# Which queue issues the score gathers: SyncE and GpSimd trade their DMAs, and the pacing copies go

## The chip, the cores and the metric

One core of one Trainium2 chip. The metric is the device time of the whole program in microseconds (us); the profiled execution also gives the span from its first to its last recorded instruction. TensorE, VectorE, ScalarE, GpSimd and SyncE are PE, DVE, ACT, POOL and SP in the profile.

## What is computed

Attention with talking heads (4 batches, 12 heads, 448 positions, head size 64), and behind it a bilinear feed-forward block on 1792 tokens (768 to 1536 and back):

```python
scores = scale * np.matmul(q, k.transpose(0, 1, 3, 2))
scores = np.einsum('bhij,hg->bgij', scores, w_pre)
scores = scores - np.max(scores, axis=-1, keepdims=True)
attn = np.exp(scores)
attn = attn / (np.sum(attn, axis=-1, keepdims=True) + 1e-09)
attn = np.einsum('bhij,hg->bgij', attn, w_post)
attn_out = np.matmul(attn, v)
a = x @ w_a
b = x @ w_b
return a * b @ w_out
```

## The kernel before, in words

**Chunks and units.** A batch's 448 queries are cut into chunks of 120, 120, 120 and 88. For a chunk, `qk` (L249) multiplies q and k head by head, and ACT copies each pair of heads from PSUM into the score tile `s` of the chunk (L266): query on the partition, then head, then key. Six such copies fill a chunk. The pool `big` holds two `s` tiles, so the copies for chunk c overwrite the tile of chunk c-2.

A chunk is then worked off in units of 20 queries (23 units a batch, 92 in all, numbered from 0). Mixing the heads wants head and query together on the partition, so `gather` (L271) moves 5 queries by 12 heads from `s` to 60 partitions of a tile `sb` by a DMA inside SBUF: four DMAs of 105 KB for a unit of 20. Each `sb` tile has AH + 1 = 4 buffers.

**A step** works on unit s: `premix` (L292; PE, 8 matmuls of L303), maximum and exponential (`smax`), the row sums' reciprocal folded into the second mixing weights (`norm`; L320 to L326), and `postmix` (L347) for unit s-1, whose transposed result ACT copies out (L357). Into the steps come, by a table made ahead (`items` and `after`, filled in the loop over `chunks` behind `av`), the `qk` pairs of the next chunk, the multiplication with v (`av`, L371) of a finished group of 8 units, the store of its result to `xd` (L381), the loads, and `spread_q` (L219; POOL reorders the q just loaded). At the head of step s, `gather(s + 3)` is issued. The first `qk` of a chunk comes three units ahead of the first unit of the chunk before it, so one step behind the issue of the last gather of the tile that it overwrites. Behind a batch's last chunk, which has five units, that step (s = 15, 38 and 61) has two `qk`.

**Queues.** Each engine takes its instructions in the program's order, DMA issues among them. SP issues all gathers, the first batch's k, the first two chunks' q, and the stores; POOL issues v, and the later k and q. A DMA completes on one of eight semaphores, which a queue's DMAs use in turn, so a queue has at most eight DMAs under way. `pace` (L122) puts one small POOL copy into each step that waits for `rs` of the unit before; what POOL issues behind it waits too.

Behind step 83 the feed-forward block's weights are loaded and converted (`load_raw` L433, L450 to L456), first beside the last units, then beside its matmuls (L494 to L496), which run to the end.

Of the kernel before, what the change touches and what calls it, by code (L numbers as in the profile page):

```python
# [7 lines left out]
F32 = mybir.dt.float32  # L8
# [13 lines left out]
def talking_heads_bilinear_kernel(  # L22
# [11 lines left out]
    nc = tc.nc  # L34
    B, _, G, S = k.shape
    H, D = 2 * G, 64
# [5 lines left out]
    QG = 3  # L42
# [49 lines left out]
    const = ctx.enter_context(tc.tile_pool(name="const", bufs=1))  # L92
# [23 lines left out]
    def ps_t():  # L116
        return ps.tile([128, 2, 512], F32, tag="t", name="pst", bufs=1)[:, 0]

    tick = const.tile([128, 1], F32, name="tick")
    seen = {}  # L120

    def pace(u):  # L122

        if u in seen:
            nc.gpsimd.tensor_copy(tick[:60], seen.pop(u)[:60, :1])  # L125

    todo_at, now = {}, [0]

    def later(fn, n=3):
        todo_at.setdefault(now[0] + n, []).append(fn)  # L130
# [56 lines left out]
    kt, qraw, qt, vt = {}, {}, {}, {}  # L187
    st, sbt, mt, at, ant, ptt, pps, xps = {}, {}, {}, {}, {}, {}, {}, {}

    def load_v(b, i):  # L190

        g, slot = divmod(i, V_PARTS)
        if slot == 0:
            vt[b, g] = v_p.tile([128, H // 2, R, D], F32, tag=f"v{g}", name="v")
        runs = [(2 * C * slot, 0, 2 * C)] if slot < R - 1 else [(2 * C * slot, 0, C), (2 * C * slot, C, C)]
        for s0, p0, n in runs:
            while n:
                r, p = divmod(s0, P)
                m = min(n, P - p)
                nc.gpsimd.dma_start(out=vt[b, g][p0:p0 + m, :, slot], in_=v[b, g][p:p + m, :, r])  # L200
                s0, p0, n = s0 + m, p0 + m, n - m

    def load_k(b, i):
        t = k_p.tile([128, S], F32, tag="k", name="k")
        (nc.sync if b == 0 else nc.gpsimd).dma_start(out=t, in_=k[b, :, i])
        kt[b, i] = t

    def load_q(c, j):
        b, t0, n = chunks[c]
        t = q_p.tile([128, QG, CHUNK], F32, tag="qraw", name="qraw", bufs=3)[:, :, :n]  # L210
        sl = slice(G * t0 + QG * j * n, G * t0 + QG * (j + 1) * n)
        (nc.sync if c < 2 else nc.gpsimd).dma_start(out=t, in_=q[b, :, sl].rearrange("d (h t) -> d h t", h=QG))
        qraw[c, j] = t

    def cut(n):
# [52 lines left out]
    def halves(n):  # L268
        return [(o, min(QH, n - o)) for o in range(0, n, QH)]

    def gather(u):  # L271
        c, o, n = units[u]
        sbt[u] = [sb_p.tile([128, S], F32, tag=f"sb{e}", name="sb") for e in range(2)]
        for i, (t, m) in enumerate(halves(n)):
            r = 64 * (i // 2)
            nb = chunks[c][2] // QB
            k_ = (o + t) // QB
            r0 = 64 * (t % QB // QH)
            if k_ < nb:
                rows = st[c][r0:r0 + QH * nb].rearrange("(i k) h s -> k i h s", k=nb)[k_]  # L280
            else:
                rows = st[c][r0 + QH * nb:r0 + QH * nb + m]
            nc.sync.dma_start(out=sbt[u][i % 2][r:r + m * H], in_=rows)

    def blocks_of(u):
        n = units[u][2]
        return [(u, j, min(QB, n - QB * j)) for j in range(2) if n > QB * j]

    def rows_of(n):
        return 64 + (n - QH) * H if n > QH else n * H  # L290

    def premix(u):  # L292
        n = units[u][2]
        tiles = sbt.pop(u)
        for k_ in blocks_of(u):
            mt[k_[:2]] = ps.tile([128, 512], F32, tag="m", name="mp")[:, :S]
        for i in (0, 2, 1, 3):
            if i >= len(halves(n)):
                continue
            m = halves(n)[i][1] * H  # L300
            r, col = 64 * (i // 2), 64 * (i % 2)
            M = 64 if n == QU or i == 0 else m
            nc.tensor.matmul(mt[u, i // 2][col:col + M], lhsT=wp[r:r + m, :M], rhs=tiles[i % 2][r:r + m])  # L303
# [12 lines left out]
    def norm(k_):  # L316
        u, j, n = k_
        m = rows_of(n)
        a, rs = at.pop((u, j))
        nc.vector.tensor_scalar(rs[:m], rs[:m], 1e-9, None, op0=ALU.add)  # L320
        if j == 0 and m > 64:
            seen[u] = rs
        rc = w_p.tile([128, 1], F32, tag="rc", name="rc", bufs=4)
        nc.vector.reciprocal(rc[:m], rs[:m])
        kr = w_p.tile([128, H, QB], F32, tag="kr", name="kr", bufs=5)
        nc.vector.tensor_scalar(kr[:m], kf[:m], rc[:m], None, op0=ALU.mult)  # L326
        ant[u, j] = a, kr
# [21 lines left out]
    def evac_p(k_):  # L349
        u, j, n = k_  # L350
        if (u, j) not in pps:
            return
        a = group_of[u]
        o = (u - groups[a][1]) * QU + j * QB
        if a not in ptt:
            ptt[a] = big.tile([128, R, H, AVC], F32, tag="pt", name="pt")
        nc.scalar.copy(ptt[a][:, :, :, o:o + n], pps.pop((u, j))[:, :, :, :n])  # L357
# [28 lines left out]
    for c in range(1, NC):  # L386
        b, t0, _ = chunks[c]
# [14 lines left out]
    for a in range(NA - 1):  # L402
        b, u0, n = groups[a]
# [6 lines left out]
    def open_moe():  # L410
        short.close()
        mo["c"] = ctx.enter_context(tc.tile_pool(name="mc", bufs=2))
        mo["w"] = ctx.enter_context(tc.tile_pool(name="mw", bufs=2))

    def load_x(b, parts=(0, 1, 2)):
        if b not in xt:
            xt[b] = big.tile([128, 2, KD, S], F32R, tag="s" if b < 2 else "pt", name="xhl")
        for i in parts:
            nc.sync.dma_start(out=xt[b].bitcast(F32)[:, 1, 2 * i:2 * i + 2], in_=xd[b][:, 2 * i:2 * i + 2])
# [10 lines left out]
    def load_raw(u):  # L430
        kind, i, e = u
        t = mo["c"].tile([128, CW, 2], I32, tag="raw", name="raw")
        nc.sync.dma_start(  # L433
            out=t.rearrange("p (k f) t -> p k (f t)", k=KD), in_=(w_ab if kind == "f" else w_out)[i, e].bitcast(I32)
        )
        raws[u] = t
# [115 lines left out]
    def take(it, n):  # L552
        for _ in range(n):
            next(it, None)
# [30 lines left out]
    def tail_ops():  # L585
        x0 = split_ops(0)
        first = conv_ops(range(2))
        for i in range(XS):
            next(first, None)
            yield  # L590
        for _ in first:
            next(x0, None)
            yield
        yield from x0

    with tc.manual_schedule():
# [30 lines left out]
        for s in range(NU + 2):  # L627
            now[0] = s
            if s == last_prep + 1:
                open_moe()  # L630
                load_raw(order[0])
                later(lambda: load_raw(order[1]), 1)
                for i in range(3):
                    later(lambda i=i: load_x(0, (i,)), 2 + i)
                tail = tail_ops()
            if s == NU - 2:
                load_x(1)
            if s == NU - 1:
                load_x(2)
            while nxt_g <= min(s + AH, NU - 1) and ready.get(units[nxt_g][0], -1) < s:  # L640
                gather(nxt_g)
                nxt_g += 1
            pace(s - 1)
            if s in (2, 4):
                for i in range(V_PARTS):
                    load_v(0, V_PARTS * (s // 2 - 1) + i)
            b, i = divmod(s, NUB)
            if b + 1 < B and 0 <= i - V_AT < 2 * V_PARTS:
                load_v(b + 1, i - V_AT)
            for fn in todo_at.pop(s, ()):  # L650
                fn()
            if s < NU:
                premix(s)
            if s >= 2:
                for k_ in blocks_of(s - 2):
                    evac_p(k_)
            if s < NU:
                for k_ in blocks_of(s):
                    smax(k_)
            pairs = [it for it in items.get(s, ()) if it[0] is qk]  # L660
            for it in items.get(s, ()):
                if it not in pairs[1:]:
                    it[0](*it[1:])
            if s < NU:
                for k_ in blocks_of(s):
                    norm(k_)
            if 0 <= s - 1 < NU:
                postmix(blocks_of(s - 1))
            for it in pairs[1:]:
                it[0](*it[1:])  # L670
            for it in after.get(s, ()):
                it[0](*it[1:])
            if s >= last_prep + 2:
                take(tail, RATE if s < NU - LATE else RATE2)
            if s == NU:
                for _ in tail:
                    pass
                tail = split_ops(1)
                for k_ in blocks_of(NU - 1):
                    evac_p(k_)  # L680
                run_a(0, 0)
            if s == NU + 1:
                run_b(0, 0)
# [59 lines left out]
        for j in range(B * KD):  # L743
            b, m = divmod(j, KD)
# [57 lines left out]
```

## Time and profile before

| | |
|---|---|
| median of 3 runs | 989.19 us (988.44 to 990.23) |
| the profiled execution | 987.99 us |
| its span | 986.2 us |
| PE busy | 926.3 us (94%) |
| DVE, ACT, POOL busy | 512.9, 412.1, 325.5 us |
| granted TensorE clock, mean | 0.973 |

PE is busy for most of the span; in a kernel like this what can be won or lost lies in the stretches in which PE waits, and in those in which its granted clock is low. So the profile is read by stretches: where PE idles, who ended that wait, and what that one waited for. A wait in the trace is put down to the semaphore that came last; as DMAs share semaphores in turn, a gather's landing can carry the name of a store.

### The profile page before, as it was taken

The numbers are of one execution on the slowest core, as the hardware profiler recorded it, in microseconds if no ns is written. First come the engines' busy times: TensorE is split into PE (matmuls) and PEld (weight loads), VectorE is DVE, ScalarE is ACT, GpSimd is POOL, SyncE is SP. The second block draws the span as 40 slices with busy tenths as digits, with TensorE's granted clock in tenths as the row PEclk, the third lists the DMA queues.
The fourth block names the chain that finished last, engine by engine and source line by source line (L and its number), as shares of the span: only waits on it lengthen the run. The fifth ranks groups of instructions, "written<-read, shape, count | busy, mean of one in ns | idle before, by whom it ended". The sixth has DMA issues, their size and how long they took to land.

```text
span 986.2 us, 20021 instructions
## 1 busy us (share of the span) xinstructions
PE 926.3 (94%) x7852; PEld 748.3 (76%) x7852; DVE 512.9 (52%) x1100; ACT 412.1 (42%) x851; POOL 325.5 (33%) x399
## 2 busy tenths in 40 slices
PE   7599699979987999979899999999999999999998
PEld 4256366646654666658799999999999999999997
DVE  3365356545654556674887555656655363341500
ACT  3467577656765768743311111111111043443521
POOL 2544113411243012020334323233332244554642
PEclk9899799989998999989999999999999999999999
DMA  4545334553355334464435424234242276656432
GB/s 143 148 146 178 123 129 146 163 161 124 127 156 189 113 132 138 148 210 157 139 133 160 146 109 150 109 140 148 96 147 109 86 259 228 223 179 246 156 124 70
DMA packets 64637, 147.60 MB, mean 150 GB/s; under 512 B 6892, under 2 KB 49024, under 8 KB 63520
## 3 DMA queue, kind: packets, MB, share of 16 engines
q1 hardware_dynamic: 58528, 131.11, 38.7%
q0 software_dynamic: 6016, 15.21, 5.7%
q8 instruction: 63, 1.03, 0.4%
q14 instruction: 30, 0.25, 0.1%
HBM read 81.01 MB, written 26.74 MB: 109 GB/s over the span
## 4 chain that ended last, share of the span: by engine, by line
PE 77%; DMA 14%; DVE 2%; ACT 2%; issue 1%; SPq 0%; POOL 0%; ACTq 0%; DVEq 0%
DMA sb<-s 9%; PE pp L347 9%; PE mp L303 7%; PE po L495 6%; PE po L496 6%; PE po L494 6%; PE xp L371 6%; PE pa L494 6%; PE pa L495 6%; PE pa L496 6%; PE pb L496 5%; PE pb L495 5%; PE pb L494 5%; PE pst L243 5%; DMA xd<-xs 4%
## 5 line engine op out<-in xcount | busy, mean ns | idle before, releaser
L347 PEld LDWEIGHTS pp<-kr,a 124*64 124x64 f32 (+1 forms) x2520 | 134.1, 139 | 47.4 <-ACT pt L357 43.9
L312 DVE TENSOR_REDUCE nm<-mp 124x1 f32<-124x448 f32 x180 | 104.3, 619 | 114.1 <-PE mp L303 112.8
L347 PE MATMUL pp<-kr,a 124*64 124x120 f32 (+1 forms) x2520 | 150.9, 272 | 3.2 <-DVE kr L326 1.7
L456 POOL TENSOR_TENSOR cvm<-cvm,cvr 128x768 int32<-128x768 int32 x36 | 66.9, 1858 | 213.3 <-DVE cvm L455 205.4
L313 ACT ACTIVATE a<-mp,nm 124x448 f32<-124x448 f32 x180 | 112.7, 631 | 56.9 <-DVE nm L312 56.8
L243 PE MATMUL pst<-k,q 64*64 64x448 f32 (+1 forms) x744 | 97.3, 575 | 38.7 <-ACT s L266 37.5
L484 POOL TENSOR_TENSOR wl<-rawo,wh 128x768 fp32r<-128x768 f32 x48 | 93.1, 1962 | 100.8 <-ACT wh L483 100.8
L506 ACT COPY sa<-pa 128x448 f32<-128x448 f32 x48 | 25.6, 533 | 223.5 <-PE pa L496 215.2
L357 ACT COPY pt<-pp 128x480 f32<-128x480 f32 x180 | 93.6, 579 | 43.9 <-PE pp L347 43.8
L266 ACT COPY s<-pst 124x896 f32<-124x896 f32 (+1 forms) x93 | 84.1, 904 | 60.6 <-DMA sb<-s 36.5
L125 POOL COPY tick<-rs 60x1 f32<-60x1 f32 x92 | 16.8, 183 | 280.5 <-DVE rs L320 280.5
L303 PE MATMUL mp<-sb,wp 60*64 60x448 f32 x720 | 101.0, 578 | 8.5 <-ACT a L313 5.4
L495 PE MATMUL pa<-xhl,wh 128*128 128x448 f32 x288 | 105.3, 366 | 1.9 <-DVE xhl L426 1.9
L494 PE MATMUL pa<-xhl,wh 128*128 128x448 f32 x288 | 105.3, 366 | 0.0
L495 PE MATMUL po<-hl,wh 128*128 128x448 f32 x288 | 104.5, 363 | 0.7 <-DVE hl L531 0.7
L496 PE MATMUL pa<-xhl,wl 128*128 128x448 f32 x288 | 105.0, 365 | 0.0
L494 PE MATMUL po<-hh,wh 128*128 128x448 f32 x288 | 104.4, 362 | 0.0
L496 PE MATMUL po<-hh,wl 128*128 128x448 f32 x288 | 104.4, 362 | 0.0
L496 PE MATMUL pb<-xhl,wl 128*128 128x448 f32 x282 | 102.3, 363 | 0.9 <-POOL wl L484 0.9
L494 PE MATMUL pb<-xhl,wh 128*128 128x448 f32 x282 | 102.2, 362 | 0.0
L495 PE MATMUL pb<-xhl,wh 128*128 128x448 f32 x282 | 102.2, 362 | 0.0
L531 DVE TENSOR_TENSOR hl<-hl,hh 128x448 fp32r<-128x448 f32 x48 | 57.5, 1252 | 75.8 <-ACT hh L530 75.8
(72 smaller groups left out, 1378.5 us busy)
## 6 DMA issues: line engine op xcount, KB each, us to landing
sb<-s SPq DMA_DIRECT2D x356, 105.0 KB
raw<-in_w_ab_dram SPq DMA_DIRECT2D x24, 768.0 KB
rawo<-wod SPq DMA_DIRECT2D x24, 768.0 KB
hd<-hf SPq DMA_DIRECT2D x48, 224.0 KB
raw<-in_w_out_dram SPq DMA_DIRECT2D x12, 768.0 KB
xhl<-xd SPq DMA_DIRECT2D x12, 448.0 KB
hl<-hd SPq DMA_DIRECT2D x4, 1344.0 KB
out_dram<-so SPq DMA_DIRECT2D x24, 224.0 KB
```

The lines of the kernel that those rows point to most:

```text
L243: nc.tensor.matmul(out[64 * e:64 * e + cols.stop - cols.start], lhsT=qt[c, i // QG][rows, i % QG, cols], rhs=kt[b, i][rows],)
L266: nc.scalar.copy(st[c].rearrange("p (g i) s -> p i g s", g=2)[:m, i], sp[:m])
L303: nc.tensor.matmul(mt[u, i // 2][col:col + M], lhsT=wp[r:r + m, :M], rhs=tiles[i % 2][r:r + m])
L312: nc.vector.tensor_reduce(nm[:m], mp[:m], axis=AXX, op=ALU.max, negate=True)
L313: nc.scalar.activation(a[:m], mp[:m], ACTF.Exp, bias=nm[:m], scale=1.0, accum_out=rs[:m])
L347: nc.tensor.matmul(o, lhsT=lhsT, rhs=rhs)
L357: nc.scalar.copy(ptt[a][:, :, :, o:o + n], pps.pop((u, j))[:, :, :, :n])
L456: lambda: nc.gpsimd.tensor_tensor(m, m, r, op=ALU.add),
L484: nc.gpsimd.tensor_tensor(ll[:, sl], raw, hh.bitcast(F32)[:, sl], op=ALU.subtract)
L494: nc.tensor.matmul(o, lhsT=hh[:, k0 + kk], rhs=mh[:, kk], start=(kk == 0), stop=False)
L495: nc.tensor.matmul(o, lhsT=hh[:, k0 + kk], rhs=ml[:, kk], start=False, stop=False)
L496: nc.tensor.matmul(o, lhsT=ll[:, k0 + kk], rhs=mh[:, kk], start=False, stop=(kk == n - 1))
```

## The change

POOL issues all gathers. SP issues every load of v, k and q. `pace` and its copies are gone, with the tile `tick` and the notes in `norm` that it used.

```diff
-    tick = const.tile([128, 1], F32, name="tick")
-    seen = {}
-
-    def pace(u):
-
-        if u in seen:
-            nc.gpsimd.tensor_copy(tick[:60], seen.pop(u)[:60, :1])
-
...
-                nc.gpsimd.dma_start(out=vt[b, g][p0:p0 + m, :, slot], in_=v[b, g][p:p + m, :, r])
+                nc.sync.dma_start(out=vt[b, g][p0:p0 + m, :, slot], in_=v[b, g][p:p + m, :, r])
...
-        (nc.sync if b == 0 else nc.gpsimd).dma_start(out=t, in_=k[b, :, i])
+        nc.sync.dma_start(out=t, in_=k[b, :, i])
...
-        (nc.sync if c < 2 else nc.gpsimd).dma_start(out=t, in_=q[b, :, sl].rearrange("d (h t) -> d h t", h=QG))
+        nc.sync.dma_start(out=t, in_=q[b, :, sl].rearrange("d (h t) -> d h t", h=QG))
...
-            nc.sync.dma_start(out=sbt[u][i % 2][r:r + m * H], in_=rows)
+            nc.gpsimd.dma_start(out=sbt[u][i % 2][r:r + m * H], in_=rows)
...
-        if j == 0 and m > 64:
-            seen[u] = rs
...
-            pace(s - 1)
```

On POOL, from the first q reordering in the set-up into the first steps, before:

```order
L226 COPY q<-qraw 128x3x60 x2
L212 DMA qraw<-in_q_dram 128x360
L226 COPY q<-qraw 128x3x60 x2
L125 COPY tick<-rs 60x1 x2
L200 DMA v<-in_v_dram 112x6x64
L200 DMA v<-in_v_dram 16x6x64
L200 DMA v<-in_v_dram 96x6x64
```

and now (the changed kernel's lines have other numbers: L275 is the gather's DMA, L218 the reordering of q, L192, L197 and L204 load v, k and q, L371 is the store):

```order
L218 COPY q<-qraw 128x3x60 x2
L275 DMA sb<-s 60x1x448 x16
L218 COPY q<-qraw 128x3x60 x2
L275 DMA sb<-s 60x1x448 x8
L218 COPY q<-qraw 128x3x60 x2
L275 DMA sb<-s 60x1x448 x12
L218 COPY q<-qraw 128x3x60 x2
```

The reorderings of q (`COPY q<-qraw`) now stand between gathers, and no load and no pacing copy is left on POOL.

On SP, over the first stores of a finished group, before:

```order
L283 DMA sb<-s 60x1x448 x64
L381 DMA xd_84<-xs 128x3x160
L283 DMA sb<-s 60x1x448 x8
L381 DMA xd_84<-xs 128x3x160
L283 DMA sb<-s 60x1x448 x17
```

and now:

```order
L204 DMA qraw<-in_q_dram 128x360
L192 DMA v<-in_v_dram 80x6x64
L192 DMA v<-in_v_dram 48x6x64
L371 DMA xd_84<-xs 128x3x160
L197 DMA k<-in_k_dram 128x448 x2
L192 DMA v<-in_v_dram 64x6x64 x2
L204 DMA qraw<-in_q_dram 128x360
L197 DMA k<-in_k_dram 128x448
L371 DMA xd_84<-xs 128x3x160
```

A store that waits for its data now holds up loads; before it held up gathers.

The semaphores that POOL's first gathers wait for, now (DMASW0 to DMASW7 are the eight on which POOL's DMAs complete in turn):

```order
L275 DMA sb<-s 60x1x448 [waits DMASW3_49]
L275 DMA sb<-s 60x1x448 [waits DMASW4_49]
L275 DMA sb<-s 60x1x448 [waits DMASW5_49]
L275 DMA sb<-s 60x1x448 [waits DMASW6_49]
L275 DMA sb<-s 60x1x448 [waits DMASW7_49]
```

Each gather waits for the landing of POOL's eighth DMA before it.

## Rows read from the trace of the kernel before

**Rows 1.** Windows: us, busy PE, PEld, DVE, ACT, POOL (xinstructions), granted clock, DMA share, GB/s.

```profile
16.08:138.51 122.43, 98.36 (x1204) 59.27 (x1204) 57.75 (x184) 72.36 (x159) 40.71 (x89) 0.92 0.48 144
138.51:244.54 106.03, 97.67 (x1292) 63.21 (x1291) 57.10 (x186) 71.42 (x160) 30.31 (x73) 0.95 0.47 147
244.54:350.20 105.66, 97.65 (x1292) 62.76 (x1290) 57.09 (x186) 71.44 (x160) 30.30 (x73) 0.95 0.46 147
350.20:410.89 60.69, 60.65 (x840) 39.53 (x839) 37.05 (x122) 45.65 (x105) 8.54 (x30) 1.00 0.39 135
...
410.89:446.57 35.68, 28.85 (x351) 19.90 (x349) 27.68 (x75) 20.78 (x51) 9.50 (x11) 0.90 0.65 213
...
500.00:986.00 486.00, 481.41 (x2406) 451.09 (x2404) 237.53 (x276) 109.52 (x182) 189.51 (x99) 1.00 0.43 151
```

**Rows 2.** Waits of the whole span: total us, times, longest us.

```profile
PEld pst L243 <- ACT s L266: 63.0, 42, 8.5
...
ACT s L266 <- DMA sb<-s: 36.5, 7, 11.2
...
ACT s L266 <- DMA xd<-xs: 8.1, 1, 8.1
...
DVE cvm L450 <- DMA raw<-in_w_ab_dram: 3.1, 1, 3.1
```

**Rows 3.** Premixes on PE: the first, and those that begin steps 38, 39, 40, 61.

```profile
17.74 1.42 PE L303 MATMUL mp<-sb,wp 60*64 60x448 f32 x5 [0.72 <-DMA sb<-s]
...
203.29 0.98 PE L303 MATMUL mp<-sb,wp 60*64 60x448 f32 x8
...
214.28 1.71 PE L303 MATMUL mp<-sb,wp 60*64 60x448 f32 x8
...
218.51 0.98 PE L303 MATMUL mp<-sb,wp 60*64 60x448 f32 x8
...
309.64 0.98 PE L303 MATMUL mp<-sb,wp 60*64 60x448 f32 x8
```

**Rows 4.** ACT around 206 us: the copy into `s` and what it waited for.

```profile
206.25 0.20 ACT L313 ACTIVATION_READ_ACCUMULATOR a<-mp,nm 124x1 f32 x1
211.77 0.91 ACT L266 COPY s<-pst 124x896 f32<-124x896 f32 x1 [5.32 <-DMA sb<-s]
```

**Rows 5.** SP's issues in order of time, merged; then all gathers' issue in ns.

```profile
377.38 20.92 SPq L283 DMA_DIRECT2D sb<-s  x24
...
192.39 11.01 SPq L283 DMA_DIRECT2D sb<-s  x8
...
L283 SPq DMA_DIRECT2D sb<-s x360: 720/737/1592, 13.1 to 432.1; - x180
```

**Rows 6.** The chain of waits at 33 us, and windows as in rows 1.

```profile
32.83 13.89 DMA sb<-s
...
33.55:46.75 13.20, 4.43 (x44) 2.05 (x44) 3.71 (x10) 2.10 (x6) 5.41 (x9) 0.83 0.51 142
...
192.39:203.40 11.01, 11.01 (x160) 7.47 (x156) 7.41 (x23) 7.88 (x20) 4.82 (x11) 1.00 0.71 211
...
377.38:398.30 20.92, 20.92 (x294) 13.92 (x292) 13.67 (x47) 17.14 (x40) 3.76 (x15) 1.00 0.38 132
```

**Rows 7.** POOL's own DMA issues (ns min/median/max), landing of q, and copies (mean ns).

```profile
L136 POOL DMA_DIRECT2D wrep<-in_w_pre_dram x2: 631/718/804, 1.5 to 2.3; - x2
...
L200 POOL DMA_DIRECT2D v<-in_v_dram x64: 526/674/828, 25.9 to 301.7; - x64
...
L212 POOL DMA_DIRECT2D qraw<-in_q_dram x28: 537/570/776, 11.3 to 381.6; - x28
...
DMA to landing us min/median/max: 2.6/5.5/9.7
...
L226 POOL COPY q<-qraw 128x180 f32<-128x180 f32 (+1 forms) x60 | 26.6, 477 | 5.3 <-DMA qraw<-in_q_dram 5.3
```

## The prediction

> **What bounds the kernel now.** I read the windows by stage first [rows 1]. From 500 us on, the feed-forward block keeps PE busy for 481.41 of 486.00 us at full granted clock, and nothing there is touched by the change. So all that can be won lies before. The stretches of the first three batches and of the last units show PE idle for 24.07, 8.36, 8.01 and 6.83 us (length less PE busy), 47.3 us in all, at a granted clock of 0.90 to 0.95. The row between them is the yardstick: the first 15 steps of the fourth batch (350.20 to 410.89) take 60.69 us with 0.04 us of PE idle at clock 1.00. They issue gathers as the others do; what is missing is the loads of a next batch.
>
> The waits say who ends the idle time [rows 2]. PE waits for ACT's copies into the score tile `s` (the row of 63.0 us, many small pieces among them that cost nothing). ACT in turn waits for gathers: 36.5 us in seven waits, and 8.1 us in one that carries a store's name; the copy reads and writes nothing of the store, but overwrites a tile whose last gather must have landed. The steps show what such a wait does: step 38 runs from 203.29 to 214.28, 10.99 us [rows 3], and ACT sat idle for 5.32 us of it [rows 4].
>
> Why is the gather late? Undisturbed, SP issues one every 0.87 us (20.92 us for 24), with 0.737 us as the median issue; beside loads eight take 11.01 us [rows 5]. The chain of waits has a gather issued at 32.83 that landed 13.89 us later; in that stretch PE was busy for 4.43 of 13.20 us, and the DMA engines were busy only 0.51 of the time, with 142 GB/s [rows 6]. Elsewhere 211 GB/s were moved. So the gathers lag although the 16 engines together are half idle: each gather reads 5 partitions, and it looks as if it sat on a few engines, in line behind its own kind and beside POOL's loads.
>
> **The change, part by part.** *The waits of ACT.* 44.6 us are on record (36.5 + 8.1). The seventh wait under the gathers' name falls in the fourth batch, where PE did not idle; I take 1 us off for it: 43.6 us. Each of the other seven is a PE stall nearly one to one, and the clock adds to it: behind the wait of step 38 the premix takes 1.71 us where others take 0.98, and step 39 is still 4.23 us long [rows 3]. Against that, in the first 15 steps of batches 1 and 2 one wait lies each, and they lose only 64.78 - 60.69 = 4.1 and 65.10 - 60.69 = 4.4 us against the yardstick (138.51 to 203.29, 244.54 to 309.64) [rows 1, 3], a little less than those two waits. So a wait costs its length and between -0.5 and +1.7 us; I take +0.5, 3.5 us for seven. Together 47.1 us, about the 47.3 us of PE idle time, some of which (the start, the last units) is of another kind.
>
> Do they all go? A tile's last gathers are issued in step s and the copy that overwrites it comes in step s+1. POOL can begin the four of a unit when the premix of step s-1 has freed their buffers, about 4.05 - 0.98 = 3.1 us before premix s (the mean step is 60.69 / 15 = 4.05). POOL's DMAs cost it 0.57 to 0.72 us in the median; the nearest in shape is the 60-partition load of a weight, 0.63 to 0.80 [rows 7]. Four at 0.65 take 2.6 us, so the last begins 1.1 us before premix s. The copy is due 206.45 - 203.29 = 3.2 us behind premix s+1 [rows 3, 4], 7.2 us behind premix s. So a landing of up to 8.3 us costs nothing. POOL's loads land in 2.6 us alone, 5.5 in the median, 9.7 in the worst case [rows 7], that last one beside the crowd that the change dissolves. I take 5.5: no wait is left. At 9.7 each of 14 overwritten tiles would cost 1.4 us, 20 us in all; that is the other end.
>
> *The last units* (410.89 to 446.57). There DVE waits 3.1 us for a weight load [rows 2] that stood behind gathers in SP's queue; now it stands behind none. I take these 3.1 us of the stretch's 6.83 us of idle time [rows 1]; 0 and 6.83 are the ends, since DVE's conversions fill this stretch (27.68 of 35.68 us busy).
>
> *The start.* From the same first issue at 13.1 us [rows 5] the four gathers of unit 0 now need 4 x 0.65 us of issue and at least 2.6 us to land, 5.2 us. On SP the first premix went on at 17.74 us, when the last it waited for had landed [rows 3], 4.6 us behind that issue. I take 1 us lost, 0 to 4 as ends.
>
> *Edits at nothing.* SP's issues lose 360 gathers and gain 110 loads. SP is hardly the bound any more; a load behind a store that waits for its data has three or four steps before its use (KL, LQ), 12 us, and a gather no longer stands there. If that cover were gone, `qk` would wait for k. POOL loses the pacing copies and loads and gains 360 x 0.65 = 234 us; in a mean step that is 2.6 of 4.05 us, and a reordering of q (two copies of 0.477 us [rows 7]) fits beside it, due only in the next step. Without `pace`, loads start as soon as buffers allow; the q buffers, freed by POOL's reorderings, hold them near their old places.
>
> Sum: 47.1 + 3.1 - 1.0 = 49.2 us off the profiled execution's 987.99 us gives 938.8, say **939 us**. That execution is 1.2 us under the median of the runs, less than what is left open here.
>
> **A rule against it.** The row [rows 6] has half-idle DMA engines beside a gather that takes 13.89 us. The Trainium skill, DMA: Bandwidth & Descriptors, section "Issuing engines are not separate DMA queues", says that DMAs run on the same 16 engines whoever issues them, and that another queue saves only issue time; by it the waits stay and the sum is 988. The trace agrees that SP's issue is not what lags, but not that the engines are full. The same page, in "Why a DMA increments its semaphore by 16 and not by 1", has a copy use k engines, k dividing both sides' outer sizes (here 5 and 60, so 5), the lowest-numbered ones from SP, a rotating set from GpSimd; by that the landings would be short and the sum stays 939. No row names an engine.
>
> **The rivals.**
> - *The crowd moves with the gathers.* While the next batch loads, gathers from POOL land as late as POOL's slowest load did, 9.7 us. For: v, k, q and the stores still move the same bytes. Against: SP's loads are cut in small pieces, and the gathers need not queue behind 13 us of their own kind. The time is 939 + 20 = 959 us.
> - *The waits stay.* The landing is bound where both queues meet. Then POOL's loss and gain cancel: 986 to 990 us. Against it stands the DMA share of 0.51 to 0.71 while gathers lag [rows 6], and the mean 0.38 where they don't.
> - *Slower: eight under way are too few.* A ninth DMA from POOL waits for the first to land, so two units take a landing and an issue. The mean step from 16.08 to 446.57 is 430.49 / 91 = 4.73 us; two steps less 0.65 are 8.8 us. If gathers land later than 8.8 us throughout, POOL's queue becomes the pace of every step. At 9.7 us a step is 5.2 us: 91 x 0.45 = 41 us more, 1029 us. For: the worst row of 9.7. Against: the median of 5.5, and a gather has fewer bytes (105 KB) than those loads (132 to 180 KB).
>
> **How the numbers follow.** The forecast has 0.73, with 930 to 950 us (all 47.3 us of idle time and 10 us of clock on one side, the start's 4 us and some lateness on the other); the crowd that moves 0.13, up to 978; waits that stay 0.06; slower 0.08. The range of 930 to 964 us takes most of the first two. Within 0.2% of before, about what a measurement of this kernel can tell from no change, is half of the third: 0.03. Faster by more has 0.73 + 0.13 + 0.03 = 0.89, slower by more 0.08.
>
> **What would show it.** Right: ACT's waits for gathers near 0 of 44.6 us; steps 4, 15, 38 and 61 of 3 to 5 us; the first 15 steps of batches 1 and 2 at 60.7 us, with clock 1.00; POOL's gathers at 0.6 to 0.7 us an issue, landing in 3 to 6 us; DVE's wait for the weight gone. Wrong: PE waits spread evenly over all steps with POOL's gathers 1.1 us or more apart (the eight under way), or the same long waits at the same steps (the engines), or a premix that waits for `sb`.

## The result, and the profile after

| | before | after |
|---|---|---|
| median of 4 runs | 988.82 us (987.21 to 990.23) | 945.88 us (943.69 to 949.99) |
| ratio, 95% interval | | 0.9571 (0.9535 to 0.9607) |
| the profiled execution, its span | 987.99, 986.2 us | 949.99, 948.3 us |
| PE, DVE, ACT, POOL busy | 926.3, 512.9, 412.1, 325.5 us | 921.6, 510.0, 412.5, 447.4 us |
| granted TensorE clock, mean | 0.973 | 0.987 |

The forecast was 939 us, its range 930 to 964. Timed again in 6 runs, the changed kernel took 945.61 us in the median, 942.01 to 949.36, ratio 0.9567 (0.9535 to 0.9599). Its executions lie up to 8 us apart (those of before, timed beside the last of these, up to 11 us: 985.97 to 997.12), and two of them are read here: the one of 949.99 us and, below, the one of 942.01 us.

From the page of the first: packets, POOL's gathers, and their landing.

```profile
DMA packets 98524, 147.79 MB, mean 156 GB/s; under 512 B 54380, under 2 KB 79488, under 8 KB 97408
...
L275 POOL DMA_DIRECT2D sb<-s x360 | 207.6, 585 | 147.2 <-ACT s L258 57.8
...
sb<-s POOLq DMA_DIRECT2D x356, 105.0 KB, 4.8
```

A gather costs POOL 585 ns in the mean and lands in 4.8 us in the median. The waits that answer to those of before [rows 2] (total us, times, longest us):

```profile
PEld pst L235 <- ACT s L258: 32.6, 42, 2.5
...
POOL sb L275 <- DMA sb<-s: 21.5, 19, 4.0
...
PEld mp L295 <- DMA sb<-s: 6.4, 6, 2.2
...
ACT s L258 <- DMA sb<-s: 5.1, 4, 2.2
```

ACT waits 5.1 us for gathers, where 44.6 us stood before; DVE's wait for the weight (3.1 us) is off the list. POOL now waits 21.5 us in 19 places because eight DMAs are under way, mostly beside other work.

The windows by stage (us; busy PE, PEld, DVE, ACT, POOL with instructions; granted clock, DMA share, GB/s), cut where the same units begin as in [rows 1]; the start is cut once more, at the premix of unit 4:

```profile
5.00:18.39 13.39, 9.09 (x114) 5.15 (x112) 5.21 (x15) 2.72 (x3) 5.42 (x10) 1.00 0.77 203
18.39:43.21 24.82, 21.48 (x173) 8.53 (x173) 9.10 (x32) 12.35 (x26) 13.46 (x26) 0.72 1.22 169
43.21:122.21 79.00, 76.43 (x1035) 49.23 (x1033) 46.22 (x153) 60.20 (x133) 51.08 (x96) 1.00 0.70 164
122.21:217.56 95.35, 94.25 (x1293) 61.54 (x1291) 56.27 (x186) 71.50 (x160) 59.51 (x111) 1.00 0.75 164
217.56:315.46 97.90, 95.83 (x1293) 62.04 (x1291) 56.84 (x186) 71.53 (x160) 59.63 (x111) 0.98 0.74 159
315.46:376.15 60.69, 60.65 (x840) 39.52 (x839) 36.96 (x122) 45.56 (x105) 36.51 (x69) 1.00 0.41 128
376.15:409.18 33.03, 29.50 (x350) 20.64 (x348) 28.56 (x74) 20.79 (x51) 18.36 (x22) 0.95 0.83 234
```

The same two stretches of the start in the kernel before:

```profile
5.00:16.08 11.08, 8.90 (x113) 4.95 (x111) 5.22 (x15) 2.72 (x3) 2.53 (x6) 1.00 0.49 153
16.08:36.13 20.05, 16.31 (x172) 7.48 (x172) 9.12 (x32) 12.22 (x26) 7.71 (x16) 1.00 0.50 137
```

Three stages are what the forecast wanted: batches 1 and 2 shrink from 106.03 and 105.66 to 95.35 and 97.90 us, and units 4 to 22 from 102.38 to 79.00. One stage went the other way: the start lost 43.21 - 36.13 = 7.1 us, at a granted clock of 0.72, with a DMA share of 1.22. A share above 1 can't be the time for which 16 engines are busy: it adds up the times of all packets, which can overlap on an engine. So a share is an upper bound on how busy the engines are, and no count of busy engines. SP's issues in that stretch, merged (start, length, count), show what is new there:

```profile
8.62 6.67 SPq L192 DMA_DIRECT2D v<-in_v_dram  x8
15.39 0.55 SPq L204 DMA_DIRECT2D qraw<-in_q_dram  x1
15.98 9.19 SPq L192 DMA_DIRECT2D v<-in_v_dram  x8
28.44 0.39 SPq L204 DMA_DIRECT2D qraw<-in_q_dram  x1
28.87 6.10 SPq L192 DMA_DIRECT2D v<-in_v_dram  x6
36.87 0.39 SPq L204 DMA_DIRECT2D qraw<-in_q_dram  x1
37.30 7.01 SPq L192 DMA_DIRECT2D v<-in_v_dram  x6
```

Before, the first v was issued at 25.9 us [rows 7]; now sixteen pieces of it go out between 8.62 and 25.2, around the first gathers. PE's rows there (idle before, and who ended it):

```profile
18.39 1.37 PE L295 MATMUL mp<-sb,wp 60*64 60x448 f32 x2 [2.14 <-DMA sb<-s]
20.32 1.76 PE L295 MATMUL mp<-sb,wp 60*64 60x448 f32 x4 [0.56 <-DMA sb<-s]
22.83 1.01 PE L295 MATMUL mp<-sb,wp 60*64 60x448 f32 x1 [0.75 <-DMA sb<-s]
...
28.61 1.71 PE L295 MATMUL mp<-sb,wp 60*64 60x448 f32 x8
```

PE waits 3.45 us for unit 0's gathers, 2.14 us of it ahead of the first premix. The premix of unit 1 then takes 1.71 us where 0.98 is usual [rows 3]: the granted clock of 0.72 for this stretch means that a little over half of it ran at the lower of the two levels, 1.2 instead of 2.4 GHz. From unit 0 to unit 4 PE is busy for 21.48 us instead of 16.31, which is 5.2 us for the same matmuls, more than the 4.8 us by which that stretch grew. The other 2.3 us are the first premix, 18.39 instead of 16.08.

### The profile page after: what moved, and what is told of

Same layout as the page of the kernel before. It is cut to its first block, busy times and chain, and to the rows that moved or that the text cites. A ratio compares the mean times of both kernels' runs of the same rounds, so it can differ in the third digit from the quotient of the medians.

```text
span 948.3 us, 19876 instructions
## 1 busy us (share of the span) xinstructions
PE 921.6 (97%) x7852; PEld 745.3 (79%) x7852; DVE 510.0 (54%) x1100; ACT 412.5 (43%) x851; POOL 447.4 (47%) x557
## 2 busy tenths in 40 slices
DMA packets 98524, 147.79 MB, mean 156 GB/s; under 512 B 54380, under 2 KB 79488, under 8 KB 97408
## 4 chain that ended last, share of the span: by engine, by line
PE 77%; DMA 6%; POOL 6%; issue 5%; DVE 3%; ACT 1%; ACTq 0%; POOLq 0%; DVEq 0%
PE pp L337 9%; DMA sb<-s 6%; PE xp L361 6%; PE po L485 6%; PE po L486 6%; PE po L484 6%; PE pa L484 6%; PE pa L485 6%; PE pa L486 6%; PE pb L486 6%; PE pb L485 6%; PE pb L484 6%; PE mp L295 6%; POOL sb L275 5%; PE pst L235 5%
## 5 line engine op out<-in xcount | busy, mean ns | idle before, releaser
L275 POOL DMA_DIRECT2D sb<-s x360 | 207.6, 585 | 147.2 <-ACT s L258 57.8
L347 ACT COPY pt<-pp 128x480 f32<-128x480 f32 x180 | 93.7, 580 | 43.7 <-PE pp L337 43.5
L235 PE MATMUL pst<-k,q 64*64 64x448 f32 (+1 forms) x744 | 95.0, 561 | 9.1 <-ACT s L258 7.2
L506 DVE TENSOR_TENSOR hf<-pb,sa 128x448 f32<-128x448 f32 x47 | 29.3, 624 | 124.7 <-PE pb L486 112.6
```

Source lines behind the costliest of these rows:

```text
L235: nc.tensor.matmul(out[64 * e:64 * e + cols.stop - cols.start], lhsT=qt[c, i // QG][rows, i % QG, cols], rhs=kt[b, i][rows],)
L275: nc.gpsimd.dma_start(out=sbt[u][i % 2][r:r + m * H], in_=rows)
```

## The experiments

The theory to be tested: gathers from SP sit on five of the 16 engines, always the same ones, and lag where a batch's loads go through these too; moving the gathers is what wins, and v's early loads are what is lost. Its rivals: SP's issue is the limit; the loads' place is what wins; the pacing copies are.

**The gathers alone moved** (in the kernel before)

```diff
-            nc.sync.dma_start(out=sbt[u][i % 2][r:r + m * H], in_=rows)
+            nc.gpsimd.dma_start(out=sbt[u][i % 2][r:r + m * H], in_=rows)
```

> Before, with the gathers alone moved to GpSimd (loads and pacing copies stay on GpSimd). Theory A (a gather from SyncE sits on 5 of 16 DMA engines, the same ones each time, behind POOL's loads; from GpSimd it does not): ACT's 44.6 us of waits for gathers fall under 12 us, unit 4 begins by 38 us since the v loads keep their late place, and the time is 938 to 955 us. Theory B (the loads have to leave GpSimd's queue): the waits stay above 25 us and the time is above 965 us.

959.72 us (955.64 to 963.84), ratio 0.9712 (0.9675 to 0.9749): between the two expectations. ACT's waits fell as the first of them said; unit 4 begins at 39.67, later than its 38. Its waits, and POOL's loads of v:

```profile
PEld pst L243 <- POOL q L226: 13.0, 7, 3.6
...
ACT s L266 <- DMA sb<-s: 4.6, 3, 1.9
```

```profile
28.82 5.39 POOL L200 DMA_DIRECT2D v<-in_v_dram  x8
```

The waits for gathers are all but gone with this one edit (4.6 us of 44.6). A new one came: eight loads of v hold POOL for 5.39 us, gathers and reorderings of q stand behind them, and PE waits for q. So the second edit, the loads to SP, is needed to free POOL.

**The loads alone moved**

```diff
-                nc.gpsimd.dma_start(out=vt[b, g][p0:p0 + m, :, slot], in_=v[b, g][p:p + m, :, r])
+                nc.sync.dma_start(out=vt[b, g][p0:p0 + m, :, slot], in_=v[b, g][p:p + m, :, r])
...
-        (nc.sync if b == 0 else nc.gpsimd).dma_start(out=t, in_=k[b, :, i])
+        nc.sync.dma_start(out=t, in_=k[b, :, i])
...
-        (nc.sync if c < 2 else nc.gpsimd).dma_start(out=t, in_=q[b, :, sl].rearrange("d (h t) -> d h t", h=QG))
+        nc.sync.dma_start(out=t, in_=q[b, :, sl].rearrange("d (h t) -> d h t", h=QG))
```

> Before, with the loads of q, k and v alone moved to SyncE, gathers on SyncE too. Theory A: the gathers stay on their 5 engines and now also stand behind loads in one queue; waits stay, 985 to 1010 us. Theory B (loads out of GpSimd's queue and its large packets are what helps): 945 to 965 us.

990.83 us (989.65 to 993.29), ratio 1.0032 (1.0016 to 1.0048). The loads' place by itself wins nothing: PE's wait for ACT stays.

```profile
PEld pst L243 <- ACT s L266: 62.4, 42, 9.5
```

**Without the pacing copies**

```diff
-            pace(s - 1)
```

> Before without the pacing copies, nothing moved. Theory A: POOL's loads come earlier, in denser crowds, the waits for gathers stay; 983 to 1000 us. Theory C (the pacing copies themselves cost the time that the change won): 945 to 960 us.

989.43 us (987.89 to 992.16), ratio 1.0016 (1.0000 to 1.0032): the same time, but not the same course. POOL's first loads of v, and the windows of units 0 to 4 and 4 to 23:

```profile
12.98 5.27 POOL L200 DMA_DIRECT2D v<-in_v_dram  x8
...
17.78:51.31 33.53, 27.05 (x173) 10.87 (x173) 9.50 (x32) 12.78 (x26) 24.49 (x45) 0.69 0.63 163
51.31:141.54 90.23, 80.36 (x1035) 51.00 (x1033) 44.89 (x152) 60.09 (x133) 10.41 (x21) 0.94 0.41 133
```

Without `pace`, v is issued from 12.98 instead of 25.88 us, unit 4 begins at 51.31 instead of 36.13, and units 4 to 22 take 90.23 instead of 102.38 us. Later on steps 38 and 61 fall to 5.68 and 5.95 us, but steps 32 and 55, right behind the next batch's v (issued between 156 and 175 us for step 32), take 12.29 and 12.39. The long waits move with the loads, and the copies had a use: they kept v away from the start.

**k and v loaded once** (the kernel before; SP issues all gathers; the later batches compute with the first one's k and v)

```diff
+        if b:
+            vt[b, i // V_PARTS] = vt[0, i // V_PARTS]
+            return
...
+        if b:
+            kt[b, i] = kt[0, i]
+            return
```

> The kernel before with k and v loaded for the first batch only and used for all four; it leaves out 18 loads of k and 48 of v, so it computes something else in the batches behind the first. SP still issues all gathers. Theory (SP's gathers sit on a few engines, and lag only where a batch's loads move through the same ones): ACT's waits for gathers go from batches 1 and 2 and the stretch 138.51 to 350.20 shrinks to near 2 x 98 us or less, in all 965 to 975 us; the start and its waits (steps 0 to 4) stay. Rival (SP's issue, 0.72 to 0.88 us for each of four gathers a unit, is what makes them late): the waits at steps 38 and 61 stay at 5 us and more and the time stays at 983 to 990.

952.25 us (950.97 to 954.51), ratio 0.9633 (0.9597 to 0.9669), more than the theory had asked for, since the loads of batch 1 are missing already in batch 0. The premixes of units 38 and 39 show what becomes of step 38, which took 10.99 us [rows 3]:

```profile
186.82 0.98 PE L309 MATMUL mp<-sb,wp 60*64 60x448 f32 x8
191.64 0.93 PE L309 MATMUL mp<-sb,wp 60*64 60x448 f32 x8
```

4.82 us, with gathers from SP as before. SP's issue is not what makes them late; they are late where k and v load beside them. Step 4, beside which the first batch's v still loads, stays at 15.91 us.

**Gathers by themselves, read from m partitions** (nothing else of the program is left; neighbouring partitions; this and the next are read from one execution each)

```diff
+        for eng, m in ((nc.sync, 4), (nc.sync, 5), (nc.sync, 8), (nc.sync, 10), (nc.gpsimd, 5), (nc.gpsimd, 4)):
+            for i in range(N):
+                eng.dma_start(out=sb[i][:m * H], in_=st[m * (i % 8):m * (i % 8) + m])
```

> Gathers alone, by themselves, and nothing else of the program: six stages of 16 DMAs inside SBUF, each from m partitions of s to 12 m partitions of sb, 21.5 KB for each partition read; first from SP with m of 4, 5, 8 and 10, then from POOL with m of 5 and 4; a stage begins when the one before has landed. It leaves out all of the computation. Theory (a gather from SP sits on m of the 16 engines, always the same ones, one from POOL on others each time): SP's stages have a DMA share near 4/16, 5/16, 8/16 and 10/16, so 0.25, 0.31, 0.50 and 0.63, and last about the same time, since each engine has as many bytes in all four; POOL's stages have a clearly higher share than SP's of the same m, 0.5 or more, and are shorter unless POOL's issue of 0.58 us each sets their length (16 x 0.58 = 9.3 us). Rival (the queue or the issue limits SP, whatever engines it uses): SP's stages last longer with m, in proportion to the bytes, at one rate in GB/s, and POOL's of m = 5 move about the same GB/s as SP's.

Windows inside SP's stages with m of 4, 5, 8 and 10 (us, length; busy DVE, POOL; clock, DMA share, GB/s):

```profile
15.00:35.00 20.00, 0.93 (x1) 0.00 (x0) 1.00 0.24 47
45.00:70.00 25.00, 0.00 (x0) 0.00 (x0) 1.00 0.26 62
77.00:105.00 28.00, 0.00 (x0) 0.00 (x0) 1.00 0.46 91
113.00:143.00 30.00, 0.00 (x0) 0.00 (x0) 1.00 0.56 118
```

The share rises with m, a little under m/16, and the GB/s with it, so no one rate limits SP. But 62 GB/s for m = 5 is half of what the program's gathers move, and POOL's stage of m = 5 ran beside the writing of the output and says nothing (the end of SP's window of m = 10 has a little of it too). So once more, with partitions as far apart as the program's (12) and the output written behind the last stage; against the run above:

```diff
-                eng.dma_start(out=sb[i][:m * H], in_=st[m * (i % 8):m * (i % 8) + m])
+                eng.dma_start(out=sb[i][:m * H], in_=st[:12 * m].rearrange("(j n) h s -> n j h s", n=12)[i % 12])
```

> The gathers alone once more, six stages of 16, with two things changed: the m partitions that one gather reads are 12 apart, as in the program, not neighbours, and the output is written only behind the last stage, so that POOL's stages are alone. It leaves out all of the computation. Theory (SP's gather on m of the 16 engines): the DMA shares of SP's stages still rise with m, near 0.25, 0.31, 0.5 and 0.6, at about equal lengths; with partitions 12 apart a gather takes 0.78 to 0.9 us as in the program, not the 1.8 us of neighbours, so that a stage lasts 13 to 16 us. POOL's stages have a share of 0.5 or more at m = 5 and are limited by POOL's issue (0.58 us each, 9.3 us and a landing). Rival (an engine takes 1.8 us for 21.5 KB here whatever the addresses): SP's stages last 31 to 37 us as before, and the 0.78 us of the program has another reason.

The same windows, and behind them POOL's with m of 5 and 4:

```profile
8.00:20.00 12.00, 5.54 (x13) 0.00 (x0) 1.00 0.25 96
25.00:37.00 12.00, 0.00 (x0) 0.00 (x0) 1.00 0.32 121
42.00:54.00 12.00, 0.00 (x0) 0.00 (x0) 1.00 0.51 192
60.00:72.00 12.00, 0.00 (x0) 0.00 (x0) 1.00 0.66 252
76.00:88.00 12.00, 0.00 (x0) 8.79 (x16) 1.00 0.62 126
93.50:105.00 11.50, 0.00 (x0) 9.00 (x16) 1.00 0.60 110
```

From SP the share is close to m/16 (0.25, 0.31, 0.50, 0.63), which is what m engines with one packet each would give. A stretch of the kernel before with gathers alone (15 to 25 us) has the same 0.32 and 119 GB/s. From POOL the packets take about twice the time in all (0.62 against 0.32), but no more bytes move (126 against 121 GB/s): alone, a gather gains next to nothing by its queue. Nor are the packets alike; those of the two stages of m = 5, from SP and from POOL:

```profile
DMA packets 875, 1.45 MB, mean 121 GB/s; under 512 B 65, under 2 KB 875, under 8 KB 875
...
DMA packets 1123, 1.51 MB, mean 126 GB/s; under 512 B 843, under 2 KB 843, under 8 KB 1123
```

From SP all are under 2 KB; from POOL 280 of 2 to 8 KB carry most of the bytes. Whether POOL's gathers keep clear of the loads by other engines or by larger packets, no run tells. The expectation that POOL's issue would set the length there (9.3 us and a landing) failed: that stage took 16.2 us, SP's 16.1.

**v's first loads later** (in the changed kernel)

```diff
-            if s in (2, 4):
+            if s in (6, 7):
                 for i in range(V_PARTS):
-                    load_v(0, V_PARTS * (s // 2 - 1) + i)
+                    load_v(0, V_PARTS * (s - 6) + i)
```

> The changed kernel with the first batch's v loads put behind step 5 instead of steps 2 and 4, so that SyncE cannot issue them before the q of chunk 3. Theory D (v loads issued at 8.6 to 25 us crowd the first gathers, which is the 7 us that the changed kernel loses before unit 4): unit 0 begins by 17.5 us, unit 4 by 38 us, and the time is 4 to 7 us under the changed kernel's, a ratio to before of 0.950 to 0.953. Rival E (GpSimd's landings are slow at the start by themselves): unit 4 at 41 us or later and the ratio stays at 0.957.

945.37 us (943.37 to 946.37), ratio 0.9564 (0.9541 to 0.9587). The start came back (unit 4 begins at 35.91), and what follows gave it away (35.91 to 121.64 lasts 85.73 us, not 79.00), so the time is not the 4 to 7 us less that was expected. SP's issues show the new crowd, batch 1's v behind batch 0's, ahead of a load of q:

```profile
24.11 23.06 SPq L192 DMA_DIRECT2D v<-in_v_dram  x22
47.28 1.95 SPq L204 DMA_DIRECT2D qraw<-in_q_dram  x1
```

**The later batches' v alone, later in their batch** (the changed kernel)

```diff
-    V_AT = 6
+    V_AT = 13
```

> The changed kernel with the later batches' v six or seven steps further back in their batch (V_AT 13 instead of 6) and the first batch's v where they were. It tells the first batch's crowd from the next batch's. Theory: the start is late because of the first batch's own 14 or so pieces of v before and at step 0 to 4; unit 4 begins at 42 to 43 us as in the changed kernel, and the time stays at 943 to 948. Rival: what SP has ahead of the first batch's needs is batch 1's v, issued early because nothing holds it: then unit 4 begins at 36 to 38 us and the time is 937 to 941.

943.05 us (942.33 to 946.36), ratio 0.9547 (0.9516 to 0.9578). Unit 4 begins at 39.35, between the two expectations, but also between the 43.21 above and the 38.66 of the changed kernel's other execution (at the end of this section). So this run doesn't tell whether batch 1's v has a part in the late start; in the changed kernel its first piece goes out at 28.87 us, behind the late first premix at 18.39. What it does change is behind unit 4: steps 4 and 6 take 3.25 and 3.33 us here, and 4.45 and 4.16 in the changed kernel.

**Both** (V_AT = 13, and the first batch's v at steps 6 and 7 as above)

> The changed kernel with two loads of v moved: the first batch's from steps 2 and 4 to steps 6 and 7, and every later batch's half a dozen steps further back in its batch (V_AT 13 instead of 6), so that the two groups do not meet on SP's queue as they did when only the first was moved. Theory: the changed kernel's start is late by about 7 us (unit 4 begins at 43.21 instead of 36.13) because v's small pieces run ahead there and share the engines with k, q and the first gathers; with the first batch's v alone moved the start came back (unit 4 at 35.91) but steps 9 and 10 gave it away, since 22 v loads stood in a row. Spaced out, the start comes back and steps 9 and 10 stay near 4 to 5 us: 936 to 940 us, 0.947 to 0.951 of the kernel before. Rival: the first batch's v is then simply too late for its first use, wherever the next batch's stand: steps 9 and 10 still take over 7 us each and the time stays at 943 to 947. Second rival: the later v's collide with the next batch's own work: steps 35 to 38 grow, the gain of the start is lost there.

941.28 us (940.07 to 941.38), ratio 0.9520 (0.9493 to 0.9546), just above what was expected. Its windows: unit 0 to 4, then batches 1 and 2:

```profile
16.81:36.48 19.67, 15.84 (x173) 7.42 (x173) 9.01 (x32) 12.11 (x26) 15.18 (x29) 1.00 0.89 176
...
116.41:211.61 95.20, 94.24 (x1292) 61.54 (x1290) 56.53 (x186) 71.17 (x160) 59.40 (x111) 1.00 0.70 164
211.61:306.81 95.20, 94.25 (x1292) 61.55 (x1290) 56.85 (x186) 71.16 (x160) 59.55 (x111) 1.00 0.69 164
```

The start is back, at full clock. But step 9 still takes 7.20 us, behind q (1.43 us of PE idle behind POOL's reordering) and not behind v, as the first rival had it.

**Half of it earlier** (V_AT = 13, and two loads of the first batch's v in each of steps 4 to 7)

```diff
-            if s in (2, 4):
-                for i in range(V_PARTS):
-                    load_v(0, V_PARTS * (s // 2 - 1) + i)
+            if 4 <= s <= 7:
+                for i in range(2):
+                    load_v(0, 2 * (s - 4) + i)
```

> The changed kernel with the later batches' v at the later steps (V_AT 13) and the first batch's v at steps 4 to 7, two loads in each instead of four in each of 6 and 7; on SP's queue that puts half of it ahead of one load of q and half behind it. With all of it behind, step 9 took 7.20 us because q came late (1.43 us of PE idle behind POOL's reordering); with all of it ahead, unit 0's and 1's gathers landed late (unit 4 at 39.35 instead of 36.48). Theory: half and half, unit 4 begins near 37.5 and step 9 takes 5.5 us; the time is 938 to 942, no more than 2 us below the run with steps 6 and 7, which a measurement can hardly tell. Rival: step 9 is late for the v itself; it stays at 7 us and the time at 941 to 944.

942.54 us (941.72 to 946.36), ratio 0.9518 (0.9478 to 0.9557). Step 9 took 5.50 us, but unit 4 began at 38.49 and step 4 took 5.27: no more is won.

**v from POOL, the rest as changed**

```diff
-                nc.sync.dma_start(out=vt[b, g][p0:p0 + m, :, slot], in_=v[b, g][p:p + m, :, r])
+                nc.gpsimd.dma_start(out=vt[b, g][p0:p0 + m, :, slot], in_=v[b, g][p:p + m, :, r])
```

> The changed kernel with v's loads on POOL, where they were before; q and k stay on SP, the gathers on POOL, no pacing copies. Theory: what the start loses is v running ahead on SP; from POOL v comes behind the gathers of its step, so unit 4 begins at 36 to 39 us. But eight v loads cost POOL 5.4 us in a row ahead of a step's gathers and reorderings, as in the run with the gathers alone moved: steps 3, 6 and 9 take 6 to 8 us, and the time is 944 to 956. Rival: v's 256-byte pieces from SP are what slows the changed kernel in the loads of every batch; then steps 3, 6 and 9 are near 4 to 5 us and the time is 932 to 940.

964.73 us (962.18 to 966.22), ratio 0.9757 (0.9726 to 0.9788), slower than both expected. Unit 4 begins at 37.31, as expected with v off SP, but steps 6 and 9 take 8.68 and 6.54 us. Steps 15, 38 and 61 take 10.94, 9.71 and 9.38 us again, and not only because of POOL's time: ACT waits for gathers once more.

```profile
94.87 0.91 ACT L258 COPY s<-pst 124x896 f32<-124x896 f32 x1 [5.29 <-DMA sb<-s]
```

In the run with the gathers alone moved, v, k and q stood on POOL as well, but behind the pacing copies, and ACT waited 4.6 us for gathers. That the missing pace makes the difference was not tried. Packets under 512 B are 29804 here and 54380 with v from SP; the cut into small pieces costs less than v on POOL does.

**The changed kernel again**

> The changed kernel itself, timed in more rounds, to set the versions with other steps for v beside it. Theory: 945 to 947 us, 0.954 to 0.958 of the kernel before, so that moving v (0.952) is worth 0.2 to 0.6%. Rival: 0.952 or less, the versions cannot be told apart.

945.61 us, as told above. The windows of its profiled execution, the shortest of its runs (942.01 us): units 0 to 4, 4 to 23, batch 1, batch 2.

```profile
17.50:38.66 21.16, 17.66 (x173) 7.90 (x173) 9.04 (x32) 12.33 (x26) 13.94 (x27) 0.92 1.20 182
38.66:118.82 80.16, 76.42 (x1034) 49.25 (x1032) 46.19 (x153) 60.13 (x133) 51.05 (x96) 1.00 0.70 162
118.82:214.02 95.20, 94.25 (x1292) 61.54 (x1290) 56.25 (x186) 71.25 (x160) 59.53 (x111) 1.00 0.72 164
214.02:309.22 95.20, 94.25 (x1292) 61.55 (x1290) 56.68 (x186) 71.22 (x160) 59.43 (x111) 1.00 0.74 164
```

The start loses 38.66 - 36.13 = 2.5 us here instead of 7.1, at clock 0.92 instead of 0.72, and batch 2 has no stall. The two versions with both groups of v moved (0.9520 and 0.9518) are 0.5% lower, but the intervals of the ratios overlap (0.9493 to 0.9546 and 0.9478 to 0.9557 against 0.9535 to 0.9599): probably better, not settled.

## Why the prediction was right, and where it was off

The terms of the sum against the changed kernel's two profiled executions (949.99 and 942.01 us), each beside the profiled execution of before, from the beginnings of the same units:

| us won | forecast | in 949.99 | in 942.01 |
|---|---|---|---|
| ACT's waits (units 4 to 68) | 47.1 | 41.8 | 43.5 |
| the last units | 3.1 | 2.6 | 2.7 |
| the start (to unit 4) | -1.0 | -7.1 | -2.5 |
| first 15 steps of batch 3 | 0 | 0.0 | 0.0 |
| behind the last unit | 0 | 0.5 | 2.2 |
| sum | 49.2 | 37.9 | 45.9 |

*ACT's waits: right, and the mechanism with it.* Batches 1 and 2 end at 95.20 us each where nothing else disturbs them, 10.8 and 10.5 us won; the shortest units 4 to 22 of any run (V_AT = 13) take 76.97 us, 25.4 won. Together 46.7, against 47.1. That fits a price of a wait's length and half a microsecond of clock; single waits were not priced. The changed kernel itself leaves 2.0 and 3.2 us of the 25.4, in steps 4 and 6, beside v's loads, and in one execution 2.7 us in batch 2. The run with k and v loaded once shows that it is the loads beside them that make SP's gathers late, and not SP's issue; that a gather sits on a few engines stays an inference.

*The landing: right in the median, in part by luck.* 2.4 to 10.6 us, median 4.8, where 5.5 was taken and 8.3 was the bound; the issue was 0.58, not 0.65. The 5.5 was the row of q's loads alone [rows 7], called that of POOL's loads; v's from POOL took 6.2 in the median, 5.0 to 9.9, and nothing said that a gather would be like the one or the other. The landings above 8.3 cost little here (ACT's 5.1 us). Steps 4, 15, 38 and 61 took 4.45, 4.80, 4.94 and 6.19 us, the last outside the 3 to 5 that was forecast (4.79 in the other execution). The first 15 steps of batch 1 took 60.69 (122.21 to 182.90), the yardstick itself.

*The last units: right within 0.5 us.* 33.03 instead of 35.68, and DVE's wait for the weight is gone.

*The start: the step that failed.* "I take 1 us lost, 0 to 4 as ends" priced the gathers' own issue and landing, and that price was fair: with v out of their way unit 0 begins at 16.26 and 16.81, 0.2 and 0.7 us late. What decided was priced at nothing, in "Without `pace`, loads start as soon as buffers allow; the q buffers, freed by POOL's reorderings, hold them near their old places". They hold q and what stands behind it; the first batch's v stands ahead, and sixteen pieces of it went out from 8.62 us on. The order on SP after the change would have told it: the first batch's v waits for no buffer. It was read over the first stores and not from its first instruction. The kernel before without its pacing copies shows the same step by itself, with v from POOL: v from 12.98 us, unit 4 at 51.31, 15.2 us late. And the late gathers cost through the clock as well: in one execution 5.2 us of slower matmuls behind 3.45 us of idle PE, in the other 1.35 us (17.66 us busy instead of 16.31) behind 2.68. That is why the same start lost 7.1 and 2.5 us, one far outside and one inside the ends. PE's premixes waiting for `sb` there are one of the signs of wrong that were named. Putting the first batch's v later brought unit 4 back to 35.91 and 36.48, below both executions of the changed kernel; that settles the cause.

*The rivals.* The crowd that moves with the gathers did not come: with loads from SP, ACT waits 5.1 us, not 20. ACT's waits came back in part where v was put on POOL without pace (13.1 us) and where 22 of its loads stand in a row (9.6 us). The waits that stay were refuted by the same row. Eight under way cost POOL 21.5 us, but the yardstick stretch stays at 60.69 us, so no step is paced by it.

*The rule against it.* That another queue saves only issue time (the Trainium skill, DMA: Bandwidth & Descriptors, "Issuing engines are not separate DMA queues") holds for gathers alone, 126 against 121 GB/s, and for the loads moved alone, 0.3% slower. It does not hold for gathers beside loads: moving them alone took 2.9% off the whole time, and SP's issue was not what made them late. The rule of k engines on the same page ("Why a DMA increments its semaphore by 16 and not by 1") agrees with SP's shares of m/16. An estimate from the rows: if four gathers of 0.87 us [rows 5] fill five engines, they do so for 3.5 us of a mean step's 4.05, and little is left there for loads; from POOL the share is about twice as high, which more engines would explain, but so would packets that overlap. No row names an engine, so that POOL's gathers go to others each time stays an inference, and why gathers lag again with v on POOL is open.

## What to carry to other kernels

A low DMA share does not mean that a transfer has room: compare it with the share that this transfer has when it is alone. Gathers that read m partitions, issued from SP, showed about m/16 alone, and were late beside bulk loads; here GpSimd for the gathers gave most, and SyncE for the loads, with `pace` gone, the rest. When a change frees a queue or drops a wait, read the queue from its first instruction on for what now starts early, and give that a step to start in: PE that idles for some microseconds at a stage's start can pay again in granted clock.

## What was not expected of the hardware

- Gathers from 5 partitions move 121 GB/s when the partitions are 12 apart and 62 GB/s when they are neighbours, at shares of 0.32 and 0.26. The Trainium skill, SBUF — State Buffer, section "Door 1: The DMA port swizzle (why `[64,N]` ≈ `[32,N]`)", has four neighbouring partitions (0 to 3, 4 to 7 and so on) share one port, and by its table partitions 0, 12, 24, 36 and 48 lie on five; the two runs agree with it (4 partitions: 47 GB/s as neighbours, 96 apart).
- From POOL, alone, gathers show a share of 0.62 where SP's show 0.32, for the same GB/s: a higher share is not more bytes.
- The changed kernel's executions differ by up to 8 us for the same instructions (942.01 and 949.99): 4.6 us of it in the start, 3.8 of them in PE's busy time at granted clocks of 0.92 and 0.72.
